# A tuned RWKV, tanh-FFN and top-1 MoE kernel: token rows sent to their experts' places as they are made, and two hand-ordered steps at the start

## The chip, the cores and the metric

One core of one Trainium2 chip runs the whole program in one launch. The metric is device microseconds of one execution, the median of the runs shown. A second number, the span, is the time from the first to the last instruction of one profiled execution.

## The reference

Three layers follow each other over 3072 tokens of width 384. Everything is computed in float32, and the kernel splits operands into a high and a low part (fp32r) to keep that precision, three matmuls for one product.

```python
# 1. linear attention with decay, batch 4, 8 heads, 768 steps, head width 48
cur = einsum('bhd,bhe->bhde', u * k_t, v_t)
y_t = einsum('bhd,bhde->bhe', r_t, state + cur)
state = w * state + einsum('bhd,bhe->bhde', k_t, v_t)
# 2. a feed-forward layer, 384 -> 2048 -> 384
h = x @ w_in;  x = (h - tanh(h)) @ w_out
# 3. a top-1 mixture of 8 experts, 384 -> 1024 -> 384
logits = normalize(x) @ normalize(emb).T / tau
e = argmax(logits);  gate = softmax(logits)[e]
out = gate * (relu(x @ w1[e]) @ w2[e])
```

## The kernel before

The tokens form 24 tiles of 128, and three tiles make a block of 384 (`TB`, `TOK`). There are eight blocks. Three stages follow each other.

**Start.** Constants, the first loads and the attention of block 0 (tiles 0 to 2) stand in an order written by hand (`startup`, a manual schedule). After it, each engine's instruction order comes from a planner that simulates the program while it is built. `tc.issue_after(x)` places what is traced inside it behind `x` on `x`'s own engine. `behind` holds back what the planner orders until the last hand-ordered instructions.

**Feed-forward layer, blocks in the order 0 (first six steps), 1, 0 (the rest), 2 to 7.** One step takes 128 of the 2048 hidden columns. `ffn1` makes them (nine matmuls of 384 columns, L547), `squares` and `small_tanh` turn them into `ghi` and `glo` on ScalarE and VectorE, and `ffn2` (L562) adds their product to the block's sums, three steps later (`LAG`). The weights arrive as raw 64-bit words in `wraw`, and `convert` (VectorE, L255 to L261) and `split` (L268, L269) make them float32 halves. The attention of the next block runs between the steps (`attn_tile`): products on GpSimd, a mask on VectorE (`causal`, L419), then `values` (L445) on TensorE. When a block's sums are complete, `finish` runs in stages between the steps of the next block:

- it copies each tile's rows to `xr` (L651) and SyncE stores them in token order in the DRAM table `xs` (L653);
- it finds each token's expert, and a small matmul `pk` (L671 to L676) with running counts gives each token a place in its expert's region; `irow` (L686) holds the places;
- GpSimd scatters the token numbers to these places in the table `tab` (L697), 8 bytes each;
- after the softmax, SyncE stores the gate beside the row in `xs` (L720).

**Experts.** `order_first` picks the two experts with the most tokens from the counts at step 8 of block 7. Each expert is run once over 384 places (`wide`), and the first three experts over some more: the first expert's 128 more places go through `narrow`, the next two take 64 and 32 more into `wide`. For an expert, `places` reads its part of `tab` into `gts` (L815), `rows` gathers the rows `xs[token]` by indirect DMA on GpSimd (L798), and `columns` transposes them on TensorE (L874). `load_expert` loads the expert's weights in four parts (`eraw`, L840 and L843), through the two buffers `stg0` and `stg1`, and converts them (L851, L852). `put` scales by the gate (L883) and scatters rows to the output (L803). The first expert's transposes and its step 0 stand at steps 13 and 15 of block 7 (`COL0`), ahead of that block's last three `ffn2`. Its `narrow` comes in at its steps 6 and 7 (`NNAR`).

## Time and profile before

| what | value |
|---|---|
| median of 3 runs | 780.39 us (779.82 to 782.03) |
| the profiled execution | 780.2 us |
| its span | 778.6 us |
| TensorE busy, share of the span | 761.0 us, 98% |
| mean granted TensorE clock | 0.991 |

The profile takes one execution. "PE" is TensorE, "PEld" its weight loads, "DVE" VectorE, "ACT" ScalarE, "POOL" GpSimd, "SP" SyncE. The time of the execution is 1.6 us above its span. A clock of 1.00 is 2.4 GHz, and 0.50 is 1.2 GHz. A wait is named by the instruction that ended it.

### The profile page before, as it was taken

The numbers are of one execution on the slowest core, as the hardware profiler recorded it, in microseconds if no ns is written. First come the engines' busy times: TensorE is split into PE (matmuls) and PEld (weight loads), VectorE is DVE, ScalarE is ACT, GpSimd is POOL, SyncE is SP. The second block draws the span as 40 slices with busy tenths as digits, with TensorE's granted clock in tenths as the row PEclk, the third lists the DMA queues.
The fourth block names the chain that finished last, engine by engine and source line by source line (L and its number), as shares of the span: only waits on it lengthen the run. The fifth ranks groups of instructions, "written<-read, shape, count | busy, mean of one in ns | idle before, by whom it ended". The sixth has DMA issues, their size and how long they took to land.

```text
span 778.6 us, 16001 instructions
## 1 busy us (share of the span) xinstructions
PE 761.0 (98%) x6157; PEld 723.0 (93%) x6157; DVE 481.3 (62%) x1076; ACT 454.9 (58%) x1054; POOL 300.5 (39%) x319
## 2 busy tenths in 40 slices
PE   9899999999999999999999999999899999999996
PEld 5689899999999999999999999998889999999996
DVE  7967975786666755765755754756564445545430
ACT  5687776665656557556656666777253445544431
POOL 3743670564641750850751540132431124312311
PEclk9899999999999999999999999999999999999999
DMA  8934350344231330330232201160463345545500
GB/s 273 302 101 140 116 182 22 93 133 130 60 119 60 87 121 21 91 131 25 90 87 91 89 2 62 32 191 32 120 217 92 114 152 184 170 145 172 179 30 31
DMA packets 41831, 87.36 MB, mean 112 GB/s; under 512 B 9718, under 2 KB 21424, under 8 KB 40722
## 3 DMA queue, kind: packets, MB, share of 16 engines
q1 hardware_dynamic: 37042, 76.74, 31.3%
q0 software_dynamic: 4288, 9.51, 3.8%
q8 instruction: 50, 0.82, 0.5%
q14 instruction: 35, 0.29, 0.1%
q10 hardware_dynamic: 416, 0.00, 0.0%
HBM read 67.38 MB, written 19.40 MB: 111 GB/s over the span
## 4 chain that ended last, share of the span: by engine, by line
PE 87%; ACT 3%; issue 3%; DMA 3%; DVE 1%; SPq 1%; POOL 1%; POOLq 0%; DVEq 0%; ACTq 0%
PE acc L562 37%; PE ph L547 36%; PE py L445 5%; PE pa L414 3%; DMA eraw<-in_moe_w_dram 1%; PE pt L874 1%; DMA ktab<-xs,gts 1%; PE warm L154 1%; PE pst L466 1%; SPq L720 1%; PE ph L958 1%; PE ph L538 1%; PE accn L562 1%; ACT wq L851 1%; PE pl L294 0%
## 5 line engine op out<-in xcount | busy, mean ns | idle before, releaser
L547 PE MATMUL ph<-xt,wq 128*128 128x384 f32 (+4 forms) x1712 | 337.4, 340 | 2.1 <-ACT wt L286 1.3
L547 PEld LDWEIGHTS ph<-xt,wq 128*128 128x128 f32 x1712 | 300.5, 188 | 6.2 <-ACT wt L286 1.5
L562 PE MATMUL acc<-wq,ghi 128*128 128x392 f32 (+2 forms) x1120 | 289.0, 344 | 0.1
L562 PEld LDWEIGHTS acc<-wq,ghi 128*128 128x128 f32 (+1 forms) x1120 | 200.6, 187 | 5.0 <-issue 1.0
L562 PE MATMUL acc<-wq,glo 128*128 128x392 f32 (+2 forms) x552 | 182.7, 341 | 0.0
L599 ACT ACTIVATE z<-ph 128x384 f32<-128x384 f32 x128 | 62.6, 489 | 89.1 <-PE ph L547 88.6
L608 DVE TENSOR_TENSOR ph<-ph,z 128x384 f32<-128x384 f32 x128 | 71.8, 561 | 51.9 <-ACT z L599 51.2
L562 PEld LDWEIGHTS acc<-wq,glo 128*128 128x128 f32 (+1 forms) x552 | 103.0, 188 | 0.3
L610 ACT ACTIVATE ghi<-ph 128x384 fp32r<-128x384 f32 x128 | 62.8, 490 | 60.2 <-DVE ph L609 56.2
L615 DVE TENSOR_TENSOR glo<-ph,ghi 128x384 fp32r<-128x384 f32 x128 | 70.8, 553 | 42.6 <-ACT ghi L610 42.5
L803 POOL DMA_INDIRECT out_dram<-ob,gts x27 | 27.9, 1034 | 153.6 <-ACT ob L883 148.4
L600 ACT ACTIVATE q<-z,sb_t 128x384 f32<-128x384 f32 x128 | 78.9, 617 | 3.5
L609 DVE SCALAR_TENSOR_TENSOR ph<-q,ph 128x384 f32<-128x384 f32 x128 | 71.8, 561 | 11.8 <-ACT q L600 3.5
L612 ACT ACTIVATE mk<-z,lz_t 128x384 bf16<-128x384 f32 x128 | 77.2, 603 | 0.0
L631 DVE SCALAR_TENSOR_TENSOR glo<-ph,ghi 128x384 fp32r<-128x384 f32 (+2 forms) x56 | 30.7, 548 | 64.5 <-ACT ghi L629 64.5
L629 ACT ACTIVATE ghi<-ph 128x384 fp32r<-128x384 f32 (+4 forms) x56 | 27.4, 489 | 67.3 <-PE ph L547 67.3
L852 DVE TENSOR_TENSOR wq<-eraw,wq 128x768 fp32r<-128x768 f32 x60 | 55.3, 961 | 15.8 <-ACT wq L851 15.2
L851 ACT ACTIVATE wq<-eraw 128x768 fp32r<-128x768 f32 x64 | 50.5, 837 | 9.8 <-DMA eraw<-in_moe_w_dram 9.6
L383 POOL TENSOR_TENSOR rk<-rkv 128x384 f32<-128x384 f32 x18 | 18.4, 1021 | 91.4 <-ACT xr L651 49.6
L269 POOL TENSOR_TENSOR wq<-wraw,wq 128x768 fp32r<-128x768 f32 (+1 forms) x17 | 30.7, 1806 | 43.3 <-ACT wq L268 40.4
L402 POOL TENSOR_TENSOR am<-ident,cd 128x512 f32<-128x512 f32 x36 | 36.9, 1050 | 8.9 <-DVE cd L388 8.9
L482 POOL TENSOR_TENSOR st<-st,pw 112x384 f32<-112x384 f32 x20 | 16.7, 837 | 50.7 <-DVE st L475 35.0
(289 smaller groups left out, 897.0 us busy)
## 6 DMA issues: line engine op xcount, KB each, us to landing
eraw<-in_moe_w_dram SPq DMA_DIRECT2D x32, 768.0 KB, 4.8
rkv<-in_rows_dram SPq DMA_DIRECT2D x18, 640.0 KB, 5.7
tt<-in_cols_dram SPq DMA_DIRECT2D x22, 448.0 KB, 4.6
xd<-xt SPq DMA_DIRECT2D x8, 1152.0 KB, 6.1
wraw<-in_moe_w_in_dram SPq DMA_DIRECT2D x8, 768.0 KB, 9.0
wraw<-in_moe_w_out_dram SPq DMA_DIRECT2D x8, 768.0 KB, 9.3
xs<-xr SPq DMA_DIRECT2D x21, 192.0 KB, 2.6
rkv<-in_rows_dram SPq DMA_DIRECT2D x4, 256.0 KB, 9.8
```

The lines of the kernel that those rows point to most:

```text
L445: nc.tensor.matmul(out=self.py[32 * g:32 * g + 32, kk, :], lhsT=lhs, rhs=rhs, start=start, stop=stop)
L547: mark["ph"] = nc.tensor.matmul(out=ph, lhsT=lhs[a][:, kk, :], rhs=rhs(b, kk), start=(kk == 0 and p == 0), stop=(kk == nk - 1 and p == 2)).ins
L562: mm = nc.tensor.matmul(out=acc[t][:lhs.shape[1]], lhsT=lhs, rhs=rhs(b, i), start=(i == span[0] and p == 0), stop=(i == span[1] - 1 and p ...
L599: nc.scalar.activation(out=z, in_=ph, func=AF.Square)
L600: nc.scalar.activation(out=q, in_=z, func=AF.Square, scale=SS, bias=sb_t)
L608: nc.vector.tensor_tensor(out=ph, in0=ph, in1=z, op=ALU.mult)
L609: nc.vector.scalar_tensor_tensor(out=ph, in0=q, scalar=KC, in1=ph, op0=ALU.add, op1=ALU.mult)
L610: mark["ghi"] = nc.scalar.activation(out=ghi, in_=ph, func=AF.Copy).ins
L612: nc.scalar.activation(out=mk, in_=z, func=AF.Relu, bias=lz_t, accum_out=zx[:, step:step + 1])
L615: mark["glo"] = nc.vector.tensor_tensor(out=glo, in0=ph, in1=ghi.bitcast(F32), op=ALU.subtract).ins
L851: nc.scalar.activation(out=hi[c][:, a], in_=t[:, a], func=AF.Copy)
L852: engs[s % len(engs)].tensor_tensor(out=lo[c][:, a], in0=t[:, a], in1=hi[c][:, a].bitcast(F32), op=ALU.subtract)
```

## The change

It has four parts.

1. **Rows scattered to their experts' places.** `finish` no longer stores to `xs`. It keeps the row tiles (two of the three in other buffers, `x2t`), and when `irow` is known it scatters the rows themselves by indirect DMA on GpSimd into a new DRAM table `xe`, laid out by expert (L697's form, three per block, placed behind the last state decay on GpSimd). `rows` then reads an expert's rows as plain blocks of `xe` from SyncE, and does not need `gts`. `clear_rows` zeroes the parts of `xe` that may stay unwritten, at step 14. The 14 memsets of the row buffers go.
2. **Full 64-byte table rows.** A row of `tab` has 16 words (token number, gate, filler) in place of 2, and it is scattered when the gate is known, after the rows. The gate is read from `gts` in `put`. The first fill of `tab` is eight times as large. `FIN` says at which steps the stages of `finish` run.
3. **Next expert's first weights ahead of the last sums.** The first two parts of the second expert's weights are loaded ahead of block 7's last three `ffn2`. They are converted at steps 5 and 6 of the first expert, and the rest from step 7 (`CONV1`). The first expert's step 0 moves from ahead of these `ffn2` to behind them (`COL0` loses 15; `issue_after(mark["acc"])`, and on VectorE behind `irow`).
4. **First two steps in fixed order.** Steps 0 and 1 of block 0 (`ffn1`, `squares`), the second weight conversion, `split`, the state sums of tiles 0 and 1 and the decay of tile 3 join the hand-written order. One multiplication of the embedding moves from VectorE to ScalarE and to step 2.

```diff
-    NEARLY = 1
+    NEARLY = 2
+    CONV1 = (5, 6, 7)
+    TW = 16
-    COL0 = (13, 15)
+    COL0 = (13,)
+    FIN = {0: (3, 4), 2: (0, 1, 3, 4, 7, 10), NB: (3, 4, 6, 10)}
+    xe = dram.tile([E * REG + P, DM], F32, name="xe")
-    tab = dram.tile([E * REG + P, 2], I32, name="tab")
+    tab = dram.tile([E * REG + P, TW], I32, name="tab")
...
     def finish(j, acc, part=None):
-            nc.sync.dma_start(out=xs[n * P:n * P + P, :DM], in_=xr)
+            src.append(xr)
...
-        for t in range(TB):
-            with tc.issue_after(root) if root else ExitStack():
-                apart("tab", nc.gpsimd.indirect_dma_start(
-                    out=tab, out_offset=bass.IndirectOffsetOnAxis(ap=irow[:, t:t + 1], axis=0),
-                    in_=tokid[:, TB * j + t, :], in_offset=None))
+        def scattered(to, t, rows):
+            ins = nc.gpsimd.indirect_dma_start(
+                out=to, out_offset=bass.IndirectOffsetOnAxis(ap=irow[:, t:t + 1], axis=0), in_=rows, in_offset=None)
+            apart("tab" if to is tab else "xe", ins)
+            return ins.ins
+        yield
+        with tc.issue_after(mark["decay"]):
+            for t in range(TB):
+                mark["xe"] = scattered(xe, t, src[t])
         yield
...
-        for t in range(TB):
-            mark["gw"] = nc.sync.dma_start(out=xs[n * P:n * P + P, DM:], in_=gw[:, t, :]).ins
+        nc.vector.tensor_copy(out=tk[:, :, 0:1], in_=tokid[:, own, 0:1])
+        nc.vector.tensor_copy(out=tk[:, :, 1:2].bitcast(F32), in_=se[:, :, None])
+        for t in range(TB):
+            scattered(tab, t, tk[:, t, :])
...
-    def rows(jb, t0, t1, n):
+    def rows(jb, t0, t1):
+        row = nc.sync.value_load(sxi[0:1, jb, 0:1], min_val=0, max_val=(E - 1) * REG)
-            lastg = gather(g, gts[:m, jb, t], n).ins
+            mark["rows"] = nc.sync.dma_start(out=g[:, :DM], in_=xe[bass.ds(row + t * P, m), :]).ins
...
+    early = [ffn1([win(p, 0) for p in range(2)], columns_of(xts[0]), NK, TOK)]
+    a[0].state_product()
+    early.append(squares(early[0], a[0].state_add))
+    convert_now(True)
+    a[TB].decay_r(nc.vector)
+    mark["pool"] = split(*ready[2])[1]
+    early.append(ffn1([win(p, 1) for p in range(2)], columns_of(xts[0]), NK, TOK))
+    a[1].state_product()
+    a[2].turned()
...
+    load = raw_expert(sxi[0:1, 1, 1:2])
+    raws1 = load, [load(c) for c in range(2)]
     while pend:
         ffn2_next()
+    next(fin)
+    next(fin)
+    with tc.issue_after(mark["acc"]), tc.issue_after(mark["irow"]):
+        next(wides[0])
+    next(fin)
+    sl = sl + rows(0, TB, TB + 1)
     for _ in fin:
         pass
-    places(0, TB, TB + 1)
-    places(1, 0, TB + (KOV > 1))
     order_rest()
-    sl = sl + rows(0, TB, TB + 1, NT)
```

## Rows read from the trace of the kernel before

**Rows 1.** Windows of 20 us: busy time of each engine, clock, DMA share.

```profile
20.00:40.00 20.00, 16.68 (x155) 13.20 (x144) 18.67 (x40) 14.27 (x36) 15.12 (x11) 0.83 0.93 292
60.00:80.00 20.00, 20.00 (x207) 18.38 (x207) 17.46 (x39) 14.95 (x38) 6.49 (x4) 1.00 0.46 139
120.00:140.00 20.00, 20.00 (x202) 18.61 (x202) 10.77 (x24) 11.90 (x31) 2.68 (x2) 1.00 0.10 29
...
540.00:560.00 20.00, 18.03 (x110) 17.45 (x108) 10.28 (x61) 5.67 (x15) 7.83 (x10) 1.00 0.32 89
560.00:580.00 20.00, 16.96 (x88) 15.37 (x89) 14.55 (x32) 12.85 (x22) 6.50 (x7) 0.91 0.77 243
```

**Rows 2.** What TensorE waited for, whole span, longest first.

```profile
PE pt L874 <- DMA ktab<-xs,gts: 2.9, 1, 2.9
PE pk L671 <- DVE oh L666: 1.5, 1, 1.5
PE ph L547 <- ACT wt L286: 1.3, 1, 1.3
```

**Rows 3.** Timeline around block 7's last sums and the first expert.

```profile
534.71 1.86 POOL L852 TENSOR_TENSOR wq<-eraw,wq 128x768 fp32r<-128x768 f32 x1 [7.51 <-ACT wq L851]
...
539.57 0.69 PE L562 MATMUL acc<-wq,glo 128*128 128x392 f32 x3
541.49 0.18 DVE L666 TENSOR_TENSOR oh<-iom,mx 128x24 bf16<-128x24 f32 x1
541.73 0.18 PE L671 MATMUL pk<-oh,tri 128*128 128x8 bf16 x1 [1.46 <-DVE oh L666]
541.97 3.37 PE L547 MATMUL ph<-xt,wq 128*128 128x384 f32 x18
542.97 0.17 DVE L686 CAST irow<-row 128x3 int32<-128x3 f32 x1
...
547.76 4.36 SPq L720 DMA_DIRECT2D xs<-gw  x3
552.97 1.54 SPq L815 DMA_DIRECT2D gts<-tab  x2
554.76 1.01 SPq L840 DMA_DIRECT2D eraw<-in_moe_w_dram  x2
555.51 1.04 POOL L798 DMA_INDIRECT ktab<-xs,gts  x1 [7.16 <-DMA gts<-tab]
...
559.16 0.33 PE L562 MATMUL acc<-wq,glo 128*128 128x384 f32 x1
562.35 0.55 PE L874 MATMUL pt<-ident,ktab 128*128 128x128 f32 x3 [2.86 <-DMA ktab<-xs,gts]
...
580.27 1.68 PE L547 MATMUL ph<-xt,wq 128*128 128x448 f32 x7
```

**Rows 4.** Windows of 2 us after the second of these waits.

```profile
562.00:564.00 2.00, 1.65 (x9) 1.65 (x10) 1.72 (x3) 1.52 (x3) 0.70 (x1) 0.87 0.51 156
564.00:566.00 2.00, 2.00 (x9) 1.90 (x9) 2.00 (x5) 0.96 (x4) 0.00 (x0) 0.50 0.73 170
566.00:568.00 2.00, 2.00 (x12) 1.79 (x10) 1.66 (x7) 1.10 (x3) 0.00 (x0) 0.78 0.99 330
```

**Rows 5.** ScalarE's timeline at the start.

```profile
25.99 0.94 ACT L268 ACTIVATE wq<-wraw 128x768 fp32r<-128x768 f32 x1 [2.24 <-DVE wraw L261]
26.81 0.50 ACT L599 ACTIVATE z<-ph 128x384 f32<-128x384 f32 x1
27.18 0.66 ACT L477 ACTIVATE st<-pst 48x192 f32<-48x192 f32 x2
27.86 0.61 ACT L600 ACTIVATE q<-z,sb_t 128x384 f32<-128x384 f32 x1
```

**Rows 6.** DMA issues by line: count, KB each, median us to landing.

```profile
eraw<-in_moe_w_dram SPq DMA_DIRECT2D x32, 768.0 KB, 4.8
xs<-xr SPq DMA_DIRECT2D x21, 192.0 KB, 2.6
out_dram<-ob,gts POOLq DMA_INDIRECT x27, 3.0
```

**Rows 7.** Tiles out_dram, tab and xs: ns and us, min/median/max.

```profile
L803 POOL DMA_INDIRECT out_dram<-ob,gts x27: 923/1016/1401, 575.0 to 773.5; - x27
DMA to landing us min/median/max: 2.5/3.0/5.9
...
L697 POOL DMA_INDIRECT tab<-tokid,irow x24: 954/960/1229, 155.0 to 547.0; - x24
...
DMA to landing us min/median/max: 1.4/3.3/6.8
```

**Rows 8.** GpSimd, VectorE and TensorE on one attention tile of a middle block.

```profile
318.04 2.05 POOL L402 TENSOR_TENSOR am<-ident,cd 128x512 f32<-128x512 f32 x2
321.60 1.33 DVE L419 COPY_PREDICATED am<-cmask,pa 128x512 f32<-128x512 uint8 x2
322.48 0.96 POOL L697 DMA_INDIRECT tab<-tokid,irow  x1 [0.30 <-issue]
326.23 0.43 PE L445 MATMUL py<-tt,st 112*32 112x128 f32 x8
346.45 0.84 POOL L482 TENSOR_TENSOR st<-st,pw 112x384 f32<-112x384 f32 x1 [5.34 <-PE acc L562]
```

More of the change, by code (lines that the diff above doesn't have):

```diff
@@ L638, in finish @@
         ssq = work.tile([P, TB], F32, name="ssq")
-        gw = work.tile([P, TB, 2], F32, name="gw")
+        src = []
         for t in range(TB):
@@ L685, in finish @@
         irow = work.tile([P, TB], I32, name="irow")
-        nc.vector.tensor_copy(out=irow, in_=row)
+        mark["irow"] = nc.vector.tensor_copy(out=irow, in_=row).ins
         rn = work.tile([P, TB], F32, name="rn")
@@ L832, in load_expert, with load @@
         w2e = w2[bass.ds(ev, 1)].rearrange("o f d -> (o f) d")
+        def load(c):
+            t = work.tile([P, WN // 4], F32, name="eraw", tag=f"stg{c % 2}", bufs=1)
+            if c < 2:
+                nc.sync.dma_start(out=t.rearrange("p (k f) -> p k f", k=NK),
+                                  in_=w1e[:, c * 512:(c + 1) * 512].rearrange("(k p) f -> p k f", p=P))
+            else:
+                nc.sync.dma_start(out=t.rearrange("p (f d) -> p f d", d=DM),
+                                  in_=w2e.rearrange("(f p) d -> p f d", p=P)[:, 4 * (c - 2):4 * (c - 2) + 4, :])
+            return t
+        return load
+    def load_expert(jb, m, gate, engs=(nc.vector,)):
+        load = raws1[0] if jb == 1 else raw_expert(m)
         hi, lo = wq[2 * (jb % 2)], wq[2 * (jb % 2) + 1]
@@ L835, in load_expert @@
         for c in range(4):
[L836 to L844 removed]
+            if jb == 1 and c < 2:
+                t = raws1[1][c]
+            else:
+                with tc.issue_after(mark["rows"]) if jb > 0 else ExitStack():
+                    t = load(c)
             m = n // 2
@@ L925, in wide @@
                 ffn2(*pend.pop(0))
-            if i >= early and i % 2 == 1:
+            if i in CONV1 if jb == 0 else i % 2 == 1:
                 next(ld, None)
@@ L981, in ahead @@
         nt = TB + (jb + 1 < KOV)
[L982 to L984 removed]
+        nxt = rows(jb + 1, 0, nt)
+        if jb == 0:
+            places(0, TB, TB + 1)
+        places(jb + 1, 0, nt)
         return load_expert(jb + 1, sxi[0:1, jb + 1, 1:2], gate)
@@ L1343, in rwkv__then__tanh_ffn__then__top1_moe_kernel @@
             xt = xts[j]
-            ph = ffn1([win(p, f) for p in range(2)], columns_of(xt), NK, TOK, IDLE[i] if i < len(IDLE) else 0)
+            ph = ffn1([win(p, f) for p in range(2)], columns_of(xt), NK, TOK, IDLE[i] if i < len(IDLE) else 0) \
+                if i > 1 else early[2 * i]
             if 0 in accs and spill:
```

156 lines of the change are left out of this document (73 added, 83 removed).

## The prediction

> **What bounds the kernel now.** I read the table of windows first, over the whole span, then the list of what TensorE waited for, then the timeline around each of its waits, and last the other engines' rows at those places.
>
> TensorE is the bound. From 60 us to the end of block 7 a 20 us window shows 20.00 us of TensorE work, or nearly that, at full clock; the two rows from the middle stand for all of them [rows 1]. No other engine's time counts there, and nothing that the change moves in that stretch can save anything. Time can come only from the few windows where TensorE is idle or slow: 20 to 40 us (16.68 busy, clock 0.83), 540 to 560 (18.03) and 560 to 580 (16.96, clock 0.91) [rows 1]. The list of waits names the two long ones of the second place: 2.9 us for the gathered rows and 1.5 us for the expert choice [rows 2]. The end of the program is not touched.
>
> **Part 3, the moved step.** After block 7's last sums (539.57 + 0.69 = 540.26) TensorE stands for 1.46 us until VectorE has the one-hot `oh`, and runs `pk` at 541.73. Steps 1 and 2 of the first expert follow, 3.37 us for both, 1.69 for one [rows 3]. The change takes step 0 from ahead of the sums and puts it behind them. The work is the same, but 1.69 us of it now lies in a hole of 1.46 us. Gain: 1.46. If the planner sets `pk` first, the gain is nothing; these are the two ends, and I take 1.46, because the step is ready and nothing holds it but the sums. VectorE's half of that step is queued behind `irow`; its reader is an `ffn2` two steps later, so that costs nothing.
>
> **Part 1, the rows.** The chain before goes from `irow` (543.14) over the softmax, three gate stores on SyncE (547.76, 4.36 us with what they wait for), the table read (552.97) and the gather (555.51) to the first transpose at 562.35, 19 us in all. TensorE had nothing left from 559.49 and waited 2.86 us [rows 3]. The chain after: `irow` comes 1.69 us earlier, at 541.45, since one step fewer stands ahead of it. Three scatters of 128 rows of 1536 bytes cost GpSimd what the output scatter costs, 1.02 us each [rows 7] with 0.30 us between two [rows 8], so the last starts at 544.1 and lands 3.0 us later [rows 6], at 547.1. SyncE then reads 192 KB; the store of that size lands in 2.6 us [rows 6]: 549.7. TensorE gets to the place at 559.49 - 1.46 = 558.03. The cover is 8.3 us, and with the slowest landings of the trace, 5.9 and 6.8 us [rows 7], it is still 1.2 us. So the wait of 2.86 us goes. Four more loads for the second expert follow on SyncE and are due some matmuls later.
>
> The Trainium skill, page "SBUF — State Buffer", section "A bandwidth-pool intuition that's wrong (but worth ruling out)", speaks against putting this on GpSimd: a DMA issued there can be held while VectorE has the shared port, 620 ns becoming about 3100 ns in its example. By that the three scatters would take an estimated 7.4 us more and eat nearly the whole cover. This case's rows do not show it: the 24 table scatters took between 954 and 1229 ns [rows 7].
>
> **What follows the wait.** The granted clock falls behind that wait: 0.87, 0.50 and 0.78 in three windows of 2 us, then full again [rows 4]. TensorE had been idle before it fell. Busy throughout, it lost 2 x (0.13 + 0.50 + 0.22) = 1.70 us there. Without the wait there is no such hole, so this comes back too; the other end is that it falls anyhow, nothing gained. I take 1.70, since the 1.46 us wait did not lower the clock (540 to 560 stands at 1.00 [rows 1]) and only the longer one did.
>
> **The early weights.** The second expert's first two loads go from 554.76 to when the first expert's last part is converted and its buffer free, 536.57 [rows 3]. They land 4.8 us later [rows 6]. Their user is the second expert's step 0 at 580.27 [rows 3], so by itself this saves nothing; it takes 1.5 MB off the DMA engines just when the rows are read. While SyncE waits for that buffer only the row loads stand behind it, which are due ten microseconds later. The remaining two loads start after the conversions at steps 5 and 6, so in the worst case they land near 558 + 4.8 = 563, 17 us before their user.
>
> **Costs at nothing, and their cover.** In the middle of the program GpSimd gets three more scatters per block, 3 x 1.32 = 4.0 us. In the block shown it idles 5.34 us at one place alone [rows 8], and TensorE there is full. SyncE loses two stores per tile and is no bound. `clear_rows` writes 3.1 MB (16 x 128 rows of 1536 bytes) near 120 us, where the DMA share is 0.10 [rows 1]; at the weight loads' rate, 768 KB in 4.8 us [rows 6], that is 20 us of a quiet stretch. The table fill grows to 1.6 MB, 10 us at that rate, beside a share of 0.46 [rows 1]. Without that cover the loads behind them would come as much later, and the attention with them; I give this no price in the sum and a little chance below. Gathers on GpSimd for the later experts become loads on SyncE under a full TensorE: nothing.
>
> **Part 4, the start.** ScalarE idles 2.24 us before 25.99, waiting for VectorE's conversion, and then does step 0's square (0.50), the state copy (0.66) and the second square (0.61) [rows 5]. In the fixed order these three stand ahead of the conversion, in that idle time, and ScalarE is 1.77 us ahead from there. VectorE is fuller (18.67 of 20 [rows 1]) and loses only one small multiplication, so I do not take more than ScalarE gives: 1.8. Bounds: a planner that orders the rest anew can make one more hole like the 1.3 us one [rows 2], so -1.3; and at most all of TensorE's idle time and slow clock in that window goes, 3.32 + 0.17 x 20 = 6.7 us [rows 1].
>
> **The sum.** 1.46 + 2.86 + 1.70 + 1.8 = 7.8 us. From the profiled execution's own 780.2 that is 772.4; its 1.6 us outside the span stay. The median of the runs is 0.2 us above that execution, so I say 772.5.
>
> **Rivals.**
> - *The start gives nothing or loses* (the planner's new order behind it): 774.2 to 775.5. For it: VectorE is nearly full there.
> - *The start gives more*, as TensorE's first steps free their banks earlier: down to 767.5. For it: step 2 waits for others' results at a slow clock.
> - *The rows come late again*: scatter and load together take over 8.3 us more than worked out, so 2.86 and 1.70 stay: 777.0, and 778.8 with a start that gives nothing. This is what the rule of the Trainium skill would do here. Against it: the slowest landings of the trace still fit.
> - *Slower: GpSimd's queue holds up the attention.* GpSimd runs in order. In the block shown, `am` ends at 320.09, the mask takes 1.33 and TensorE reads at 326.23 [rows 8], so there are 4.8 us to spare. If both kinds of scatter of a block stand ahead of an `am`, 6 x 1.32 = 7.9 us, TensorE waits 3.1 us in each of the five blocks that have a following attention: 15.6 us, 788. It decides from 4.8 us of delay on. Against it: the table scatters stood behind `am` (322.48 after 318.04).
> - *No change at all* (`pk` first, rows late, start nothing): 780.2.
>
> **How the numbers follow.** Forecast as worked out, 770 to 774: 0.47. Start nothing: 0.17. Start more: 0.15. Rows late: 0.12, half of it above 778. No change: 0.03. Slower by the queue, or by a late load: 0.06. A difference within 0.3% (2.3 us) of the median cannot be told from none, so faster means below 778.0: 0.47 + 0.17 + 0.15 + 0.06 = 0.85; same 0.09; slower 0.06. The range 767.5 to 778 leaves out the slower cases and about half of the late ones.
>
> **What the profile would show.** `pk` without a wait ahead of it; the narrow tile's transposes with no DMA wait, rows landed before 552; a clock of 1.00 from 560 to 580; ScalarE without the hole at 24 to 26 us, and `ffn1` of step 2 about 2 us earlier. Wrong, if a wait for `xe` rows stands ahead of the transposes, if TensorE waits for GpSimd in the middle blocks, or if the new order leaves another hole before 100 us.

## The result and the profile after

The change made the kernel slower: median 784.72 us (781.57 to 790.34, 20 runs), against 780.39 (778.59 to 782.48, 20 runs) beside it; ratio 1.0054, 95% interval 1.0039 to 1.0069. I had said 772.5. The profiled execution took 781.89 us with a span of 780.2, so it is one of the shorter ones of the kernel, and it shows 1.6 us of the loss. Over the 20 runs the span goes from 779.9 us (mean granted clock 0.993) to 788.7 (0.981).

Line numbers of the changed kernel are 7 to 15 higher than before: `ffn1` L554, `ffn2` L569, `pk` L679 to L684, `irow` L694, the scatters L703, `columns` L889.

The list of what TensorE waited for, changed kernel:

```profile
PE pk L679 <- DVE oh L674: 4.0, 2, 2.5
PE pt L291 <- ACT ktok L367: 2.3, 1, 2.3
PE ps_cd L380 <- DVE rows L374: 1.5, 1, 1.5
...
PE py L452 <- DVE am L426: 0.6, 1, 0.6
```

The wait for gathered rows [rows 2] is gone. `pk` now waits twice, and of the waits that are new VectorE ends most; the largest exception is the 2.3 us that ScalarE ends at the start. Windows of 20 us of the changed kernel, and then the one of the kernel before that the second line is to be held against:

```profile
20.00:40.00 20.00, 16.79 (x159) 13.20 (x156) 18.69 (x41) 14.57 (x38) 13.64 (x10) 0.83 0.88 273
180.00:200.00 20.00, 16.87 (x166) 15.10 (x166) 16.23 (x45) 10.46 (x29) 10.03 (x11) 0.91 0.19 58
...
540.00:560.00 20.00, 18.55 (x114) 18.31 (x113) 13.05 (x65) 8.75 (x21) 9.14 (x11) 1.00 0.38 115
560.00:580.00 20.00, 18.96 (x109) 17.16 (x108) 13.45 (x28) 12.19 (x22) 8.28 (x11) 1.00 0.55 159
```

```profile
180.00:200.00 20.00, 20.00 (x206) 19.14 (x205) 15.45 (x43) 13.32 (x35) 10.27 (x10) 1.00 0.30 86
```

540 to 580 us is better than before [rows 1], at full clock. 20 to 40 us is as before. The loss is in a window that was full: 180 to 200 us had 20.00 us of TensorE at 1.00 before, and now has 16.87 at 0.91.

The timeline around block 7's last sums:

```profile
544.16 0.70 PE L569 MATMUL acc<-wq,glo 128*128 128x392 f32 x3
546.31 0.17 PE L679 MATMUL pk<-oh,tri 128*128 128x8 bf16 x1 [1.45 <-DVE oh L674]
...
551.52 0.96 POOL L703 DMA_INDIRECT xe<-xr,irow  x1 [0.30 <-issue]
554.08 0.34 SPq L827 DMA_DIRECT2D ktab<-xe  x1
...
565.53 0.49 PE L889 MATMUL pt<-ident,ktab 128*128 128x128 f32 x3
```

The rows are fetched from 554.08 us on and the transposes at 565.53 wait for nothing, where they waited 2.86 [rows 3]. But the planner put `pk` ahead of the moved step, so TensorE still stands 1.45 us.

The start, ScalarE and TensorE, and then step 2's products in the kernel before:

```profile
24.59 0.49 ACT L606 ACTIVATE z<-ph 128x384 f32<-128x384 f32 x1
...
32.60 0.46 ACT L367 ACTIVATE ktok<-ps_k 128x384 f32<-128x384 f32 x1
33.11 1.70 PE L291 MATMUL pt<-ident,wraw 128*128 128x128 f32 x6 [2.30 <-ACT ktok L367]
36.58 2.84 PE L554 MATMUL ph<-xt,wq 128*128 128x384 f32 x9
```

```profile
37.37 2.08 PE L547 MATMUL ph<-xt,wq 128*128 128x384 f32 x9
```

ScalarE's hole is filled [rows 5]. But TensorE now waits 2.30 us for `ktok`, which stands behind four diagonal copies on ScalarE, and step 2's products start 0.8 us earlier than before, take longer (2.84 us against 2.08) and end at 36.58 + 2.84 = 39.42 us, as before (37.37 + 2.08 = 39.45).

**Where the 1.6 us went.** A simple ruler is the place of `pk` in each block, since it follows the block's last sums. Start of the first `tri` matmul of `pk`, in us, from each trace (two kernels further down are added here):

| block | 1 | 0 | 2 | 3 | 4 | 5 | 6 | 7 |
|---|---|---|---|---|---|---|---|---|
| before | 150.7 | 191.8 | 251.6 | 313.4 | 375.2 | 436.3 | 496.6 | 541.7 |
| changed | 149.8 | 194.8 | 257.3 | 319.1 | 380.8 | 441.9 | 502.0 | 546.3 |
| norms_first | 148.3 | 190.6 | 250.5 | 315.4 | 382.0 | 443.0 | 504.3 | 548.4 |
| order_only | 148.6 | 189.4 | 249.4 | 311.1 | 372.8 | 433.9 | 494.0 | 538.3 |

The changed kernel is 0.9 us ahead at block 1, loses 3.9 to block 0 (45.0 against 41.1) and 2.7 to block 2 (62.5 against 59.8), and nothing from there to block 6 (244.7 against 245.0). Then come 0.9 more: 44.3 against 45.1 - 1.69, as step 0 no longer lies in that stretch. So it is 546.3 - (541.7 - 1.69) = 6.3 us late at the experts, and that is the sum of the stretches, -0.9 + 3.9 + 2.7 - 0.3 + 0.9. It ends 1.6 late. So 4.7 us come back there, about the 2.86 + 1.70 of the prediction.

The 0.9 us at block 1 are less than the start differs from one execution to the next: step0_first further down, which changes nothing ahead of block 7's last sums, has this `pk` at 151.6 us, 1.8 later. The stretches behind block 1 repeat better: its 44.7 and 62.6 us stand beside 45.0 and 62.5 here.

The place of the loss, VectorE, GpSimd and TensorE of the changed kernel:

```profile
174.23 0.91 POOL L699 TENSOR_TENSOR rn<-rn,half 128x3 f32<-128x3 f32 x1
175.10 1.30 POOL L353 TENSOR_TENSOR tt<-tt,tab_r 112x512 f32<-112x512 f32 x1
175.17 5.40 DVE L717 TENSOR_SCALAR rn<-rn 128x3 f32<-128x3 f32 x1 [1.10 <-POOL rn L699]
...
179.53 1.00 POOL L391 TENSOR_TENSOR rk<-rk,u_bc 128x384 f32<-128x384 f32 x1
188.75 0.62 PE L569 MATMUL acc<-wq,ghi 128*128 128x392 f32 x2 [0.46 <-DVE part L652]
191.15 0.96 POOL L703 DMA_INDIRECT tab<-tk,irow  x1 [0.30 <-issue]
194.48 0.17 DVE L729 COPY tk<-tokid 128x3 int32<-128x3 int32 x1 [1.41 <-DMA tab<-tk,irow]
194.56 0.17 DVE L674 TENSOR_TENSOR oh<-iom,mx 128x24 bf16<-128x24 f32 x1
194.79 0.17 PE L679 MATMUL pk<-oh,tri 128*128 128x8 bf16 x1 [2.53 <-DVE oh L674]
195.01 4.94 PE L554 MATMUL ph<-xt,wq 128*128 128x384 f32 x18
```

Two things hold VectorE here. An addition to three numbers per partition, `rn` plus 1e-6, takes 5.40 us and ends with GpSimd's run of attention work (179.53 + 1.00). And the copy of the token numbers into `tk`, the small table that the new 64-byte rows are scattered from, waits 1.41 us until block 1's table scatters have read `tk`; the planner had put it ahead of block 0's `oh`. `pk` waits 2.53 us, and the next 18 matmuls take 4.94 us, where such a group took 3.37 [rows 3].

The groups of these two instructions over the whole span, the changed kernel and then the one before (columns: count, busy us, mean ns, idle before and what ended it):

```profile
L717 DVE TENSOR_SCALAR rn<-rn 128x3 f32<-128x3 f32 x8 | 22.9, 2860 | 9.6 <-POOL rn L699 9.6
L729 DVE COPY tk<-tokid 128x3 int32<-128x3 int32 x8 | 5.6, 696 | 17.4 <-DMA tab<-tk,irow 16.7 <-issue 0.7
```

```profile
L706 DVE TENSOR_SCALAR rn<-rn 128x3 f32<-128x3 f32 x8 | 2.2, 269 | 0.7 <-POOL rn L691 0.2
```

### The profile page after: what moved, and what is told of

It reads as the page before. It is cut to its first block, busy times and chain, and to the rows that moved or that the text cites. A ratio compares the mean times of both kernels' runs of the same rounds, so it can differ in the third digit from the quotient of the medians.

```text
span 780.2 us, 16008 instructions
## 1 busy us (share of the span) xinstructions
PE 758.3 (97%) x6157; PEld 720.9 (92%) x6157; DVE 495.5 (64%) x1083; ACT 453.2 (58%) x1055; POOL 292.9 (38%) x313
## 4 chain that ended last, share of the span: by engine, by line
PE 84%; DVE 6%; issue 4%; ACT 2%; POOL 2%; DMA 2%; POOLq 0%; SPq 0%; DVEq 0%
PE acc L569 36%; PE ph L554 36%; PE py L452 4%; PE pa L421 3%; DVE rn L717 1%; PE pt L889 1%; PE pst L473 1%; POOL xe L703 1%; DMA tab<-tk,irow 1%; DMA rkv<-xe 1%; PE accn L569 1%; DVE ph L618 1%; POOL tab L703 0%; POOL out_dram L808 0%; PE pt L291 0%
## 5 line engine op out<-in xcount | busy, mean ns | idle before, releaser
L554 PE MATMUL ph<-xt,wq 128*128 128x384 f32 (+4 forms) x1712 | 339.3, 342 | 2.9 <-ACT wt L293 1.3
L554 PEld LDWEIGHTS ph<-xt,wq 128*128 128x128 f32 x1712 | 302.2, 190 | 7.2 <-ACT wt L293 1.5
L569 PE MATMUL acc<-wq,ghi 128*128 128x392 f32 (+2 forms) x1120 | 289.3, 343 | 0.6 <-DVE part L652 0.5
L569 PEld LDWEIGHTS acc<-wq,ghi 128*128 128x128 f32 (+1 forms) x1120 | 200.2, 187 | 5.9 <-DVE part L652 1.2
L569 PE MATMUL acc<-wq,glo 128*128 128x392 f32 (+2 forms) x552 | 182.0, 340 | 0.0
L606 ACT ACTIVATE z<-ph 128x384 f32<-128x384 f32 x128 | 62.6, 489 | 92.1 <-PE ph L554 85.6
L619 ACT ACTIVATE ghi<-ph 128x384 fp32r<-128x384 f32 x128 | 62.5, 489 | 70.0 <-DVE ph L618 65.0
L569 PEld LDWEIGHTS acc<-wq,glo 128*128 128x128 f32 (+1 forms) x552 | 102.8, 187 | 0.1
L624 DVE TENSOR_TENSOR glo<-ph,ghi 128x384 fp32r<-128x384 f32 x128 | 70.8, 554 | 44.3 <-ACT ghi L619 43.1
L703 POOL DMA_INDIRECT tab<-tk,irow x24 | 24.5, 1022 | 34.6 <-DVE tk L730 27.4
```

Of the source, the lines that this page charges most:

```text
L554: mark["ph"] = nc.tensor.matmul(out=ph, lhsT=lhs[a][:, kk, :], rhs=rhs(b, kk), start=(kk == 0 and p == 0), stop=(kk == nk - 1 and p == 2)).ins
L569: mm = nc.tensor.matmul(out=acc[t][:lhs.shape[1]], lhsT=lhs, rhs=rhs(b, i), start=(i == span[0] and p == 0), stop=(i == span[1] - 1 and p ...
L606: nc.scalar.activation(out=z, in_=ph, func=AF.Square)
L619: mark["ghi"] = nc.scalar.activation(out=ghi, in_=ph, func=AF.Copy).ins
L624: mark["glo"] = nc.vector.tensor_tensor(out=glo, in0=ph, in1=ghi.bitcast(F32), op=ALU.subtract).ins
```

## The experiments

All ratios are to the kernel before, run beside each kernel, with their 95% intervals. The medians of the kernel before lay between 779.66 and 780.45 us on these occasions, so two kernels are compared by their ratios; the difference of their medians can be off by some 0.8 us.

### Is it the one buffer of the table rows, or the place of its copy?

**two_tables** gives `tk` a second buffer (one of the two fills goes behind the decay of the starting states).

```diff
-    tk = const.tile([P, TB, TW], I32, name="tk")
+    tks = [const.tile([P, TB, TW], I32, name=f"tk{i}") for i in range(2)]
...
+        tk = tks[j % 2]
```

> The changed kernel with two buffers for the table rows `tk`, one for even and one for odd blocks; the second is filled on GpSimd after the first blocks, so that nothing is added at the start. Theory 1: in the stretch from 185 to 197 us the copy of the token numbers into `tk` waits 1.41 us for the preceding block's table scatters to have read `tk`, `oh` stands behind it on VectorE, `pk` waits 2.53 us and the clock falls to half for the next step (18 matmuls 4.94 instead of 3.3 us). Then with two buffers the copy waits for no transfer, `pk` waits under 1 us there, the granted clock of 180 to 200 us is 1.00, and the time falls by 3.5 to 5 us: 780 to 781 at the median where the changed kernel has 784.7 (ratio to the kernel before 0.999 to 1.001), with a smaller spread than 781.6 to 790.3. Rival 2: the stall comes from the work that the three added row scatters bring (GpSimd's queue, the sums with the bank put aside): the copy's wait moves to another instruction, `pk` still waits over 2 us and the ratio stays 1.004 to 1.007. Rival 3: most of the loss is at the start: the ratio stays above 1.003 although `pk`'s wait is gone.

Measured: 786.16 us, 1.0069 (1.0046 to 1.0093). No gain. VectorE waits as long as before, the second buffer notwithstanding:

```profile
DVE tk L730 <- DMA tab<-tk,irow: 15.9, 5, 5.3
```

The theory had the culprit right and the remedy wrong. The copy needs nothing but a free buffer, so the planner puts it right behind the scatter that frees one: at 197.79 us a copy into block 1's buffer, for block 3, waits for block 1's scatters, with block 0's `oh` behind it, and `pk` waits 2.1 us.

**held_copy** keeps one buffer and moves the copy behind `irow` of its own block.

```diff
-        nc.vector.tensor_copy(out=tk[:, :, 0:1], in_=tokid[:, own, 0:1])
+        with tc.issue_after(mark["irow"]):
+            nc.vector.tensor_copy(out=tk[:, :, 0:1], in_=tokid[:, own, 0:1])
```

> The changed kernel with one buffer, but the copy of the token numbers held behind `irow` of the same block on VectorE, so that it stands behind `oh` and, for the first block, no longer at 5.40 us in the starting chain. Theory 1: the copy may still wait for the scatters, but `oh` is ahead of it: `pk` waits under 1 us near 194 us and the clock holds, 3.5 to 5 us; beyond that the start's chain (the sum `ps_cd` waits 1.51 us for a product on VectorE in the changed kernel) comes back by up to 0.9 us: median 779 to 781 (ratio 0.998 to 1.001). Rival 2 (the scatters' own load): `pk` still waits over 2 us, ratio 1.004 to 1.007. If the start matters and the stall does not: about 783.8 (ratio 1.004).

Measured: 781.42 us, 1.0020 (1.0002 to 1.0037), 2.7 us under the changed kernel by the ratios (3.3 between the medians). The copy waits for no transfer any more, and in the ruler block 1 to block 2 takes 105.6 us instead of 107.5, so that 1.9 us of the gain show there. At the start TensorE waits 0.9 us for VectorE's product instead of 1.51, but step0_first, with the copy where it was, shows 0.7 there: this can't be put down to the copy. `pk` still waits 0.97 us near 194, and the list of TensorE's waits shows the next thing that VectorE delivers late, the mask at 224 us:

```profile
PE pk L679 <- DVE oh L674: 2.4, 2, 1.5
...
PE py L452 <- DVE am L426: 1.9, 1, 1.9
```

### What are the fixed order and the moved step worth in the changed kernel?

**no_fixed_start** puts back the order of the kernel before at the start (part 4 undone, the rest as changed).

> The changed kernel with the fixed order of the first two steps taken out again (the order of the kernel before; rows, table and the moved step as changed). Theory 1: the fixed order fills ScalarE's hole of 2.24 us, but TensorE then waits 2.30 us for the rows of keys that ScalarE turns, and step 2's products end at 39.42 instead of 39.45 us: it gains about nothing, so that without it the time is within 1 us of the changed kernel's (784 to 786, ratio 1.004 to 1.007), and the stall near 194 us stays. Rival: the fixed order does bring the 1.8 us of the prediction: 786.5 (ratio 1.0075 or more). Rival 3: the fixed order is itself the loss: 780 to 782.

Measured: 786.28 us, 1.0071 (1.0048 to 1.0093), 1.6 us more than with it. The intervals overlap, so this alone does not settle it. One thing in its trace bears on the clock: `pk` of block 0 waits 2.50 us here too, but the 18 matmuls behind it take 3.37 us and the clock stays at 1.00 (4.94 us in the changed kernel).

**start_alone** adds part 4 alone to the kernel before.

> The kernel before with the fixed order of the first two steps alone (the first two steps traced and put in order inside the starting part, the embedding scaled on ScalarE behind it; no other part of the change). The prediction's price: a gain of 1.8 us, 778.6 (ratio 0.9977). From the changed kernel without the fixed order (786.3 against 784.7 with it): a gain of 1.5 us (0.998). Rival: TensorE's wait of 2.30 us for the turned rows of keys comes in here as well, nothing is gained (1.000), and the order pays only beside the changed kernel's fills at the start.

Measured: 779.21 us, 0.9991 (0.9979 to 1.0003): less than the prediction's 1.8, and not told from nothing.

**step0_first** puts `pk` behind the moved step.

```diff
-    next(fin)
-    next(fin)
-    with tc.issue_after(mark["acc"]), tc.issue_after(mark["irow"]):
+    with tc.issue_after(mark["acc"]):
         next(wides[0])
+    next(fin)
+    next(fin)
```

> The changed kernel with the sums `pk` of the last block put behind the first step of the first expert on TensorE (the step held behind the last sums alone, the index chain traced after it). In the changed kernel `pk` stands ahead of that step and TensorE waits 1.45 us for `oh` at 546.3 us. Theory: the step of about 1.7 us fills that wait, the index comes 0.3 to 1.5 us later, still ahead of its use: `pk` waits under 0.3 us there and the time falls by 1.2 to 1.5 us, to about 783.3 (ratio 1.0035 to 1.005). Rival: the last block's rows or the next transposes come late by it and the transposes wait: no gain (ratio 1.0054) or a loss.

Measured: 785.65 us, 1.0062 (1.0040 to 1.0085), no gain. The wait of `pk` is gone (TensorE is full from 540 to 560 us), and it comes back further on. ScalarE takes the next weights ahead of the extra tile's `hh`, and here they were late:

```profile
575.21 1.58 ACT L866 ACTIVATE wq<-eraw 128x768 fp32r<-128x768 f32 x2 [1.18 <-DMA eraw<-in_moe_w_dram]
577.76 1.58 ACT L866 ACTIVATE wq<-eraw 128x768 fp32r<-128x768 f32 x2 [0.97 <-DMA eraw<-in_moe_w_dram]
579.24 0.58 ACT L976 ACTIVATE hh<-ph 128x512 f32<-128x512 f32 x1
579.87 1.11 PE L979 MATMUL pt<-ident,hh 128*128 128x128 f32 x4 [2.73 <-ACT hh L976]
```

### The addition that takes five microseconds

**norm_form** writes it with two tensor inputs (the sum, and the larger of sum and old value).

```diff
-        nc.vector.tensor_scalar(out=rn, in0=rn, scalar1=1e-6, scalar2=None, op0=ALU.add)
+        nc.vector.scalar_tensor_tensor(out=rn, in0=rn, scalar=1e-6, in1=rn, op0=ALU.add, op1=ALU.max)
```

> The changed kernel with one instruction in another form: the addition of 1e-6 to the row norms `rn` (128x3) on VectorE is written with two tensor inputs and one scalar (the sum, and the larger of it and the old value, which is the sum) in place of one tensor and two scalars. In the changed kernel this addition takes 2.86 us in the mean and 5.40 to 5.43 us at 175 and 216 us, while GpSimd runs five attention operations from 175.10 to 180.53 us; in the kernel before it takes 0.27 us. Other small operations with two tensor inputs take 0.18 us beside the same GpSimd work. Theory: the norms now stand directly ahead of GpSimd's attention work, so that this form of addition cannot run until GpSimd pauses, VectorE is 5 us late at 180 and 221 us, and from that come the late bank sum (two waits of 0.46 us), the late table copy (part of the 1.41 us) and the late mask (0.60 us, 1.86 in the kernel with the held copy). Then the addition takes under 0.4 us in the mean and the time falls by 1.5 to 4 us: 781 to 783 (ratio 1.001 to 1.0035). Rival: the addition waits for its input (the power on GpSimd ends later than the trace shows), so that the other form takes as long and nothing changes (1.004 to 1.007). Rival: VectorE has slack there, the addition falls to 0.2 us and the time stays.

Measured: 784.84 us, 1.0055 (1.0037 to 1.0074). Nothing changed, and the tile's view (min, median, max ns) says why:

```profile
L717 DVE SCALAR_TENSOR_TENSOR rn<-rn x8: 161/2926/5418, 178.4 to 555.9; 128x3 f32<-128x3 f32 x8
```

The other form stands as long. I had taken the wrong row as a model: the small operations that took 0.18 us ran beside GpSimd's scatters, not beside its arithmetic. The Trainium skill would have said so: page "SBUF — State Buffer", section "Who interferes with whom", has an instruction of VectorE with two inputs in SBUF contend with a GpSimd instruction that reads SBUF, and the one that comes second blocks. The trace agrees, with 2.93 us in the median: in the changed kernel the addition stands through three or five GpSimd operations in a row.

The recorded rival, that the addition only waits for its input from GpSimd, would fit this run as well. The kernel before settles it. Its cast of `irow` reads a tile of VectorE, waits for nothing of GpSimd's, and takes up to 2.5 us:

```profile
L686 DVE CAST irow<-row x8: 169/1118/2512, 153.9 to 543.0; 128x3 int32<-128x3 f32 x8
L715 DVE TENSOR_SCALAR se<-se x8: 154/169/4060, 161.0 to 547.1; 128x3 f32<-128x3 f32 x8
```

The five casts that took 0.81 us or more all lay beside GpSimd's arithmetic, the other three (0.17 us) did not; the addition of 4.06 us at 161 us lay beside it too. So VectorE stood like this before the change as well, but nothing that TensorE waited for was behind it.

**held_forms** is held_copy with this form, the same form for the addition to `se` and the cast of `irow`, and the reciprocal written straight into `tk`.

> The changed kernel with the copy of the token numbers held behind `irow` (as in the kernel with the held copy, 1.0020) and with the additions to the norms and to the sums and the cast of `irow` in the form with two tensor inputs, the reciprocal written straight into `tk`. If the held copy and the form remove different delays of VectorE, the waits of `acc` for the bank sum, of `py` for the mask and most of that of `pk` near 194 us are gone and the time is 1.5 to 3 us under that of the held copy: 778.5 to 780 (ratio 0.9975 to 0.9995). If the held copy had already taken the delay that the form would remove: 781.4 (1.002).

Measured: 780.41 us, 1.0004 (0.9989 to 1.0019), not told from held_copy, since the intervals overlap.

**held_forms_late** also moves two fills of GpSimd away from the start.

```diff
-        nc.gpsimd.iota(tk, pattern=[[1, TB * TW]], base=BIG, channel_multiplier=0)
...
-        nc.gpsimd.memset(zero, 0.0)
+        with tc.issue_after(mark["decay"]):
+            nc.gpsimd.memset(zero, 0.0)
+            nc.gpsimd.iota(tk, pattern=[[1, TB * TW]], base=BIG, channel_multiplier=0)
```

> The kernel with held copy and other forms, and also the fill of `tk` and the zeros for the rows moved on GpSimd from the start to behind the last decay of the starting states. Theory: at the start GpSimd's fills run beside VectorE's decay tables (five of them in 2.06 us in the changed kernel, 1.06 in the kernel before) and the sum `ps_cd` waits 0.9 us for them also when the copy is held; without these fills the first products come 0.3 to 0.9 us earlier and the time falls by as much: ratio 0.0005 to 0.001 below that of the same kernel without the move. Rival: the tables were slowed by the table fill `tinit`, which stays: no difference.

Measured: 779.98 us, 0.9997 (0.9983 to 1.0011), no difference: TensorE's idle time in the first 20 us was 1.42 us with the fills there and is 1.29 without. The mask at 220 us still comes 1.86 us late, and the clock of 220 to 240 us is 0.91 in this trace.

**norms_first** is that kernel with the norms' power on GpSimd ahead of the row scatters, so that VectorE's addition falls beside scatters.

```diff
         with tc.issue_after(mark["decay"]):
+            norms()
             for t in range(TB):
                 mark["xe"] = scattered(xe, t, src[t])
         yield
-        with tc.issue_after(mark["xe"]):
-            norms()
```

> The kernel with held copy, other forms and late fills (0.9997), and the power of the row norms on GpSimd put ahead of the three row scatters of its block instead of behind them. The form of the addition made no difference: with two tensor inputs it still takes 2.9 us in the mean and 5.42 us at 213 us, ending with GpSimd's run of five attention operations (213.11 to 218.55 us); after it the mask is late, TensorE waits 1.86 us for it and the granted clock of 220 to 240 us falls to 0.91, 1.8 us. Theory: an addition on VectorE with all its data in SBUF stands still while GpSimd computes, and does not while GpSimd only issues scatters; ahead of the scatters it has some 3.8 us. Then `rn` takes under 0.4 us in the mean, the wait of `py` near 220 us and the clock's fall go, and the time is 2 to 4 us lower: 776 to 778 (ratio 0.995 to 0.997). Rival: the mask is late by VectorE's other work (the wait of `py` stays over 1 us although `rn` is short): 0.9985 to 1.001. Rival: the scatters come one microsecond later and the stall moves there: 1.000 or more.

Measured: 783.60 us, 1.0044 (1.0026 to 1.0061): slower than without. Yet the step itself did what it should. The addition is short, the mask's wait is gone, and in the ruler above block 0 to block 2 takes 59.9 us (59.8 before the change, 63.8 in held_forms_late):

```profile
L716 DVE SCALAR_TENSOR_TENSOR rn<-rn x8: 149/161/163, 169.7 to 551.2; 128x3 f32<-128x3 f32 x8
```

The loss is new and lies elsewhere: block 2 to 3 takes 64.9 us (61.8 before), 3 to 4 takes 66.6 (61.8).

### The gaps that no engine explains

The timeline of norms_first in the first of these stretches, GpSimd and TensorE:

```profile
280.13 1.00 POOL L703 DMA_INDIRECT tab<-tk,irow  x1 [3.07 <-DVE tk L729]
281.43 0.96 POOL L703 DMA_INDIRECT tab<-tk,irow  x1 [0.30 <-issue]
282.16 0.28 PE L473 MATMUL pst<-rkv,ktok 128*32 128x48 f32 x4 [0.37 <-issue]
282.70 0.96 POOL L703 DMA_INDIRECT tab<-tk,irow  x1 [0.30 <-issue]
282.90 0.28 PE L473 MATMUL pst<-rkv,ktok 128*32 128x48 f32 x4 [0.46 <-issue]
283.64 0.31 PE L473 MATMUL pst<-rkv,ktok 128*32 128x48 f32 x6 [0.46 <-issue]
284.37 0.43 PE L473 MATMUL pst<-rkv,ktok 128*16 128x48 f32 x18 [0.42 <-issue]
```

"issue" says that TensorE waited for nothing that the profile shows. The gaps come every 0.73 us. They begin in the attention's short products 1.0 to 1.7 us after GpSimd has started the first of the three table scatters, and the last ends 0.7 us after the last scatter has been issued. Near 346 us it is the same (scatters at 345.36, 346.67 and 347.94, gaps from 346.65 to 349.56).

**early_finish**, **weights_first** and **early_weights** build on norms_first and have its gaps too. The first runs block 1's last stages earlier, the second issues the first expert's weight loads ahead of its row loads, the third does both (`raw` marks a weight load).

```diff
-    FIN = {0: (3, 4), 2: (0, 1, 3, 4, 7, 10), NB: (3, 4, 6, 10)}
+    FIN = {0: (3, 4, 5, 6, 7), 2: (0, 1, 3, 4, 7, 10), NB: (3, 4, 6, 10)}
```

```diff
-                sl = rows(0, 0, TB)
...
+                if i == 9:
+                    with tc.issue_after(mark["raw"]):
+                        sl = rows(0, 0, TB)
```

> The kernel with the norms first, and the last parts of block 1's end (rows and table scatters) traced in steps 5 to 7 of block 0's second half instead of all at its end, where block 0's own end follows at once. In the kernel with held copy, other forms and late fills `pk` of block 0 still waits 0.97 us for `oh` near 191 us, since VectorE does both ends together. Theory: spread apart, that wait falls below 0.3 us: 0.5 to 1 us less than with the norms first alone (ratio lower by 0.0005 to 0.0015). Rival: the rows of block 1 get in the way of GpSimd's work for block 2's attention and the masks wait: no gain or a loss.

> The kernel with the norms first, and the first expert's first two weight loads issued on SyncE ahead of its three row loads (before: behind them, by 1.7 to 2 us). In the kernel with held copy, other forms and late fills ScalarE stands 4.89 us at 511 to 516 us for these weights with the next step's square queued behind, and 520 to 540 us has 1.29 us of TensorE idle (0.06 in the kernel before). Theory: the weights land 1.5 to 2 us earlier and 0.5 to 1.3 us are gained there (ratio lower by 0.0007 to 0.0015 than with the norms first alone). Rival: the wait is for the transfer itself, shared with the row scatters; the idle time stays and nothing is gained.

> All of these together: held copy, other forms, late fills, norms first, block 1's end spread, weights ahead of the rows. If the parts add up: 774.5 to 777 (ratio 0.993 to 0.996). If the stalls share their slack (one filled, the next appears): the same as the best single one, 0.995 to 0.997.

Measured: 786.94 us, 1.0095 (1.0074 to 1.0116); 783.42 us, 1.0059 (1.0036 to 1.0082); 788.33 us, 1.0113 (1.0088 to 1.0137). In all three the gaps are the longest waits of TensorE: 4.6, 3.0 and 4.8 us in the state products alone. The wait of `pk` near 191 us, which early_finish was to take away, is gone in norms_first already; and early_finish puts block 1's table scatters at 165.53 us beside the state products of another tile, with four gaps that end from 167.57 us on. What these edits are worth by themselves can't be read here.

**table_late** is norms_first with the table scatters traced a step later and held behind the state decay, so that they should miss the short products.

```diff
-    FIN = {0: (3, 4), 2: (0, 1, 3, 4, 7, 10), NB: (3, 4, 6, 10)}
+    FIN = {0: (3, 4), 2: (0, 1, 3, 4, 7, 11), NB: (3, 4, 6, 11)}
...
-        for t in range(TB):
-            scattered(tab, t, tk[:, t, :])
+        with tc.issue_after(mark["decay"]):
+            for t in range(TB):
+                scattered(tab, t, tk[:, t, :])
```

> The kernel with the norms first (1.0044), and the table scatters of each block traced one step later and held behind the last state decay traced, so that GpSimd issues them after attention's short products and not beside them. Theory: TensorE's gaps of 0.4 us in these products (3.8 us in nine gaps, 1.1 in four, with a fall of the clock to 0.91 near 340 us) come from the scatters issued at the same time; they go, the stretch from the index sums of block 2 to those of block 3 takes 61.8 us again (64.9 with the norms first), that to block 4's 61.8 (66.6), and the time is 5 to 8 us lower: 775.5 to 779 (ratio 0.995 to 0.999). Rival: the gaps belong to the products at this place in the step order; they stay and the time stays (1.003 to 1.006). Rival: the scatters, now inside the next tile's preparation on GpSimd, make its masks late and TensorE waits for these: gaps gone, the time no better.

Measured: 775.21 us, 0.9929 (0.9909 to 0.9949), 9.0 us under norms_first by the ratios and faster than both kernels. Windows of norms_first, and then of table_late:

```profile
280.00:300.00 20.00, 18.12 (x166) 17.10 (x155) 9.15 (x17) 11.04 (x26) 9.33 (x9) 1.00 0.34 117
340.00:360.00 20.00, 17.94 (x163) 16.91 (x162) 9.74 (x21) 9.61 (x23) 11.16 (x11) 0.91 0.34 118
```

```profile
280.00:300.00 20.00, 20.00 (x191) 19.68 (x190) 11.39 (x23) 12.54 (x30) 9.33 (x9) 1.00 0.33 117
340.00:360.00 20.00, 20.00 (x190) 19.67 (x189) 11.50 (x24) 13.01 (x31) 9.33 (x9) 1.00 0.33 118
```

The scatters are still in the first of these windows, at 289.01, 290.32 and 291.58 us, but beside the long matmuls of `ffn1` and `ffn2`, and those lose nothing. So the place of the table scatters in GpSimd's order is what costs, and moving it takes the gaps away. That every meeting of table scatters and short products costs is not so. Block 1's table scatters still meet them in table_late:

```profile
184.50 1.00 POOL L703 DMA_INDIRECT tab<-tk,irow  x1 [0.15 <-issue]
186.14 0.42 PE L452 MATMUL py<-tt,st 112*32 112x128 f32 x8
187.71 0.52 PE L473 MATMUL pst<-rkv,ktok 128*32 128x48 f32 x32
```

The other two scatters follow at 185.81 and 187.08 us, and the 56 products of `values` on record and the 32 state products beside them run without a gap, here and in the four kernels below. In norms_first the same scatters stood at 181.96 us, as long ahead of the same products, with gaps of 0.34 and 0.29 us. What tells the two cases apart is not shown.

**table_late_weights** adds weights_first to it.

> The same, and the first expert's first weight loads issued ahead of the row loads. If the gaps go: 0 to 1 us lower than with the table scatters late alone (0.994 to 0.999); the waits of ScalarE near 511 us (4.89 us) shrink by 1.5 to 2 us. If the row loads come too late for the transposes near 534 us: a wait there and 1 to 3 us more.

Measured: 774.49 us, 0.9928 (0.9911 to 0.9944), no difference to table_late.

### What the parts are worth once the stalls are gone

**order_only** is the changed kernel with three edits of order alone: the copy held, the norms first, the table scatters late. The forms and fills are those of the change.

> The changed kernel with three changes of order alone: the copy into `tk` held behind `irow`, the norms' power ahead of the row scatters, the table scatters held behind the last state decay. No other forms, and the fills of `tk` and of the zeros at the start as in the changed kernel. If order alone brings the gain: 775 to 777 (ratio 0.993 to 0.996), at most 1 us above the kernel with forms and late fills (0.9929), and that from the start (0.4 us between the kernels with and without late fills). If the forms or the late fills were needed: 778 or more.

Measured: 774.98 us, 0.9944 (0.9930 to 0.9958). Order alone takes 8.6 us off the changed kernel by the ratios (9.7 between the medians). TensorE has no wait at all from 150 to 260 us.

**table_late_old_start** is table_late without part 4.

> The kernel with the table scatters late (0.9929) with the fixed order of the first two steps taken out. From the changed kernel (1.0071 without it, 1.0054 with it) and from the kernel before (0.9991 with it alone): a loss of 0.7 to 1.5 us, 776 to 777 (ratio 0.9938 to 0.995). The prediction's price of 1.8 us: 777. Rival: with the late fills the old start is as good: 775.2 (0.993).

Measured: 777.11 us, 0.9963 (0.9950 to 0.9975). The fixed order is worth 777.11 - 775.21 = 1.9 us between the medians and 2.7 us by the ratios here, and the intervals only just miss each other.

**table_late_step0** is table_late with `pk` behind the moved step (the edit of step0_first).

> The kernel with the table scatters late, with `pk` of the last block behind the first step of the first expert. `pk`'s wait of 1.46 us goes. The prediction's price: 1.46 us, 773.8 (ratio 0.991). From the changed kernel with the same edit (1.0062 against 1.0054): the gain is given back where the rows, and behind them the second half of the next expert's weights, come later, and ScalarE stands for these weights ahead of the extra tile's `hh` (2.73 us of wait there): 775 to 776 (0.9925 to 0.994).

Measured: 773.51 us, 0.9916 (0.9902 to 0.9930), the lowest of all: 1.0 us under table_late by the ratios, 1.7 between the medians, with overlapping intervals. The timeline:

```profile
538.30 1.73 PE L554 MATMUL ph<-xt,wq 128*128 128x384 f32 x9
539.92 0.18 PE L679 MATMUL pk<-oh,tri 128*128 128x8 bf16 x1
```

The step lies in the hole and `pk` follows without a wait. This time ScalarE does not stand for the second expert's weights.

## Why the prediction was wrong

**The step that failed is "Costs at nothing, and their cover", with the sentence on the bound that it rests on: "No other engine's time counts there".** It looked for cover on GpSimd (4.0 us of scatters in 5.34 us of idle time) and found it. It did not ask what the new instructions do to VectorE, whose order also sets when `oh`, the masks and the sums that were put aside (`part`) reach a full TensorE. Between block 1 and block 2 the changed kernel lost 6.6 us by this, in a stretch that the prediction had at nothing. Two things were late there. The copy into `tk`, which the part did not list at all, stood in front of `oh` waiting for a transfer; moving it alone brought 1.0054 to 1.0020 (held_copy), 1.9 us of it in this stretch. The norms stood behind the row scatters, directly ahead of GpSimd's arithmetic, so that VectorE stood up to 5.4 us on one addition. Taking that away gave block 0 to 2 its 59.9 us back, but needed the table scatters moved as well. With the three in order the changed kernel runs at 0.9944.

**The rival "GpSimd's queue holds up the attention"** had the sign and the stage but not the mechanism: the masks came late by 0.6 to 1.9 us because VectorE stood, not because `am` stood behind six scatters.

**Part 3, the moved step.** "If the planner sets `pk` first, the gain is nothing": it did. Where the order was forced, the wait of `pk` went in both kernels. In the clean one the time fell by 1.0 us by the ratios, too little to be told from nothing; in the changed one the gain was given back, through weights that arrived behind ScalarE's turn for them.

**Part 1, the rows, and "What follows the wait".** Right in the profiled pair: no wait at the transposes, clock 1.00 from 560 to 580 us, 4.7 us regained against 4.56. From block 7's `pk` to the end the changed kernel takes 233.9 us and held_copy, table_late and order_only 234.0, so this part repeats. The sum for the clock counts the window from 562 us as busy throughout, though TensorE still stood for 0.35 us of it; that is 0.05 us. The row scatters took 956 to 1197 ns, so the Trainium skill's rule on a held DMA (page "SBUF — State Buffer", the section that the prediction names), which the prediction had set against this part, does not show here either. One table scatter, at 525.34 us, took 1734 ns. The estimate by that rule, 7.4 us, was also short of the cover of 8.3 us, so by the prediction's own figures it alone would not have made the rows late, as the rival on them says.

**Part 4, the start.** 1.8 predicted; 1.9 to 2.7 in the clean kernel, 1.6 in the changed one, 0.7 on the kernel before, the last two not told from nothing. In the profiled pair step 2's products end at 39.42 us, against 39.45 before, where the prediction wanted them some 2 us earlier. ScalarE's gain is there, but up to this point it is spent again on the wait for `ktok` and on the slower products behind it. So the size came out near the prediction without the earlier step 2 that it named as a sign, and where the gain arises is not shown.

**The sum.** 7.8 us were predicted. The kernel with these stalls out of the way, which also has the late fills and the other forms, measures 0.9916, some 6.6 us of 780.4 (5.5 to 7.6 by the interval). So the gains together were sized about right and the cover was not.

**What stays open.** The median of the changed kernel lies 2.8 us above its profiled execution. Longer executions have lower mean clocks, and traces of other kernels with the same stall show the clock under 1.00 between 180 and 240 us, but which stretch was slow in the other executions of this kernel can't be seen. The start is one candidate: three windows of 20 us from 0 us on have the clock at 1.00, 0.83 and 1.00 in the changed kernel's trace, at 1.00, 0.91 and 0.91 in step0_first, and at 0.83, 0.88 and 0.95 in norm_form and two_tables, whose programs are nearly the same there; `pk` of block 1 comes at 151.6 to 153.4 us in these three, against 149.8. How a table scatter holds up TensorE's short products, and why only in some meetings, is open too. Row scatters met 8 or 16 products of `pa` in most of the traces without a gap; a meeting with state products was not seen.

## What to carry to other kernels

A new instruction on an engine that is not the bound is free only if nothing that the bound waits for is queued behind it in that engine's order; so list every small instruction that a change adds, each with its wait and with what stands behind it. A second buffer does not take a wait away if the planner simply fills it as early as it can: hold the instruction behind what must go first. And after each repair look again where the time went, since here one that worked (3.9 us between block 0 and block 2) was followed by another stall of twice its size (7.9 us between block 2 and block 4).

## What the runs showed of the hardware

- VectorE's additions of 128x3 numbers with all data in SBUF stood still while GpSimd did arithmetic, in both forms: 2.86 us in the mean, up to 5.43, and 0.16 us beside GpSimd's scatters. In the kernel before, casts of 128x3 numbers took 0.81 to 2.51 us beside GpSimd's arithmetic and 0.17 us elsewhere; reductions to 128x3 took 0.17 to 0.18 us beside it.
- TensorE's short attention products showed gaps of 0.29 to 0.46 us about each 0.73 us beside three indirect table scatters from GpSimd (norms_first); in five later traces 86 or more such products beside three of these scatters showed none. Matmuls of 384 columns beside them showed none in any.
- After a wait of 2.53 us the clock fell to 0.50 (1.2 GHz, 196 to 198 us of the changed kernel) and 18 matmuls took 4.94 us instead of 3.37. After one of 2.50 us in no_fixed_start, and after one of 1.45 us (540 to 560 us of the changed kernel), it stayed at 1.00 (2.4 GHz).
